# Plain values of two batches in 18 tiles of 128 rows, their queries in token order, sums over tiles in PSUM

## The chip, the cores and the metric

The kernel runs as one program on one core of a Trainium2 chip. The metric is device time in microseconds, median of several runs; lower is better. Three runs of the kernel before took 307.17 us in the median (306.58 to 307.39). One profiled execution gives the times of its instructions; its own time was 307.09 us, and the span from its first to its last instruction 305.2 us.

A core has five engines with queues of their own: PE (matmul), DVE (vector), ACT (activation), POOL (general) and SP, which here only issues transfers. Matmul results land in PSUM, in eight banks of 128 partitions by 512 fp32; PE, DVE and ACT reach it.

## The reference

Attention of 8 batches, 8 heads, 576 tokens and 64 dimensions, with two kinds of mask, then a two-layer product with a leaky ReLU:

```python
mask_plain = (rel >= 0) & (rel < window)                                   # window 32, heads 0 to 3
mask_dil = (rel >= 0) & (rel < window * dilation) & (rel % dilation == 0)  # dilation 4, heads 4 to 7
attn = exp(masked scores / 8), divided by its sum over keys
x = (attn @ v), heads side by side: 4608 tokens x 512
out = leaky_relu(x @ w_in) @ w_out      # w_in 512 x 2048, w_out 2048 x 512, fp32 in and out
```

A plain query sees its own token and the 31 before it; a dilated query sees 32 tokens four apart, which are 32 neighbours among the tokens of the same residue by 4.

## The kernel before, in words

**Chunks.** `x` is kept transposed in fp16 in `xt`, 1152 columns for two batches, token order by residue (column r*96 + i stands for token 4i + r). Twelve chunks of 384 columns follow each other: `up` (L1073) multiplies a chunk by `w_in` in 16 groups of four matmuls, ACT applies the leaky ReLU on the way to `gt` (L1084), and the product with `w_out` gives 128 tokens at a time. The first four such tiles are plain products (`down`, L1244, four steps of four matmuls of 512 columns); the others go in groups of four with seven products in place of eight (L1335). The last four chunks form the up product in the same way (`up_seven`, L1157). Chunks 0 and 1 are the first 384 tokens of batch 0 and of batch 1, chunk 2 the rest of both.

**Attention of batches 0 and 1** (`EARLY`) works on pairs of heads: hp 0 and 1 plain, hp 2 and 3 dilated. `load_group` loads q, k, v of four heads in fp32, casts them (L342 on ACT, L344 on the others) to `nat` and `v_all`; `turn` transposes q and k by PE (L729) and moves them from PSUM to `slots` (`move`, L646 on ACT, L648 on DVE): queries to `qbd`, where the two heads stand in halves with zeros between, so that one matmul gives both heads' scores, and keys to `kt`. Tokens are cut in part 0 (the first 384) and part 1 (the rest); the dilated heads' last tokens come by `load_rest`. `unit` does 192 queries of two heads:

- scores into one bank of `sps` or `hps` (L888; L872 for the short dilated ones). In part 0 (`BY_PE`) a matmul of the identity with a bias (L869) comes first and adds -60000 outside the mask; in part 1 a multiplication after the exponential (L905) does that;
- exponential by ACT (L894) into one of four `ee` tiles;
- values (L929, L949, L939) and sums into a bank of `ops`. In part 0 (`TILED`) one matmul gives 64 rows, head by head on the two halves of the array, and the sums come from a stationary of ones (L917); in part 1 the stationary has values and ones side by side;
- the reciprocal by ACT as exp(-ln) (L961, L963), and the normalization by DVE into `xt` (L967).

For the plain heads the queries are in blocks of 96 and each block has the 128 keys that it can see, from 32 before it. Neighbouring key blocks overlap by 32 rows, so the values are loaded in 12 pieces of 128 rows every 96 rows for each pair of heads; in a block of 96 the queries stand residue by residue. For the first block of batch 0 the rows before token 0 are filled by a memset (`t_vz`) and two extra transfers.

**Attention of batches 2 to 7** (`late_unit`, L1010 scores, L1023 exponential, L1026 mask, L1016 sums and values, L1034, L1037 reciprocal, L1045 normalization) is spread over the rest of the span; its transposes are by DVE into `turned` (L697) or `slots` (L704, L717, L722), with copies by POOL (L687).

**The order of the work** is planned. Every operation is a task with an engine (or a choice of engines), a duration assumed by the author, dependencies and a priority; `_Plan.run` places them one after the other, `latest` recomputes the priorities backward, and `SEEDS` disturbs them at random in some passes. The instructions are written out in the planned order, one in-order queue for each engine, all loads and stores on SP. `FIRST` is the order of the early loads: b and c are q, k of batches 0 and 1 (dilated heads first), v and y their values, i an eighth of `w_in`, o an eighth of `w_out`, 0 and 1 the rest of each batch. `WHEN`, `RANKS`, `MOE`, `SUMS`, `W_SUMS`, `NEAR` are times that set priorities. In gaps of the plan before 62 us PE multiplies zeros (L1558); eight such matmuls (L1454) open the program. The pieces of `w_out` are staged in `xt1`, `wst` and `gt1`, some of them twice, so that a later one waits for the casts of an earlier.

Of the kernel before, what the change touches and what calls it, by code (L numbers as in the profile page):

```python
# [19 lines left out]
WHEN = (4.52, -1.03, 5.19, 90.96, 96.86, 93.61, 150.56, 174.24)  # L20
WARM = 62.0
W_SLOW = 1.25
SEEDS = (0, 0, 0, 0, 0, 0, 0, 0, 0, 775539)
AFTER = -1495.0
NEAR = -1498.63
FIRST = 'bvbviiii0iiiicycyoooooooo1'
RANKS = ((12.88, -25.12), (25.21, -10.26), (-1.14, 23.42), (33.7, 4.07))


def _constants():  # L30
# [3 lines left out]
    key = p - 32  # L34
    c = np.arange(96)[None, :]
    qry = 4 * (c % 24) + c // 24
    rel = qry - key
    band = (rel >= 0) & (rel < WIN)
    first = band & (key >= 0)
    rel0 = c - p  # L40
    d0 = (rel0 >= 0) & (rel0 < WIN)
# [3 lines left out]
    masks = np.concatenate([d0, first, band, d2], axis=1)  # L45
# [165 lines left out]
def kernel(  # L211
# [51 lines left out]
    NBIAS, NMASK = 3 * 96 + 48, 96 + 48  # L263
    NCON = 128 + NBIAS + NMASK
    NLATE = 480 + 2 * 384
    M_D0, M_FIRST, M_BAND, M_KEEP = 128, 224, 320, 128 + NBIAS
# [92 lines left out]
    def zeros(n):  # L359
# [6 lines left out]
    t_con = add("ACT", 0.21, 0.22, [t_bias],  # L366
                lambda e: nc.scalar.activation(out=con[:, M_KEEP:NCON], in_=con[:, M_BAND:M_KEEP], func=AF.Exp),
                -700)
# [38 lines left out]
    t_vz = clear("POOL", vst[1][0:PAD, 0:D], 0.1, 0.0, -9350)  # L407
# [17 lines left out]
    def load_group(b, g, prio, prio_v):  # L425
# [39 lines left out]
        elif early:  # L465
            lv = []
            for j in range(2):
                n = 12 - (first and j == 0)
                lj = [load("SP", at(vs, 0, 128, (12 * j + 12 - n) * D, [D, n], [1, D]),
                           dram(v, base + (1152 * j + 96 * (12 - n) - 32) * D, [D, 128], [96 * D, n],  # L470
                                [1, D]), 128 * n, 256, v_old, prio_v + 0.3 * j)]
                if n < 12:
                    lj += [load("SP", at(vs, PAD, 128, 0, [1, D]), dram(v, 0, [D, 96], [1, D]),
                                96, 256, v_old, prio_v), t_vz]
                lv.append(lj)
# [18 lines left out]
        for j in range(2):  # L494
# [20 lines left out]
            n_v = 256 if dil else 384  # L515
            h_a, h_s = j * n_v, 2 * n_v
            n, w = n_v // D, 128 * (8 if dil else 6)
# [10 lines left out]
    def load_rest(b, prio):  # L528
# [5 lines left out]
        for o, src in ((0, q), (1, k)):  # L534
            lo.append(load("SP", at(st, 0, 128, o * 256, [1, 256]),
                           dram(src, b * H * HS + 512 * D, [HS, 8], [4 * D, 16], [1, 256]),
                           128, 1024, s_old, prio))
# [1083 lines left out]
```

## Time and profile before

| what | value |
| --- | --- |
| median of three runs | 307.17 us |
| the profiled execution | 307.09 us, span 305.2 us |
| PE busy | 293.0 us (96%), 3039 matmuls |
| DVE busy | 249.9 us (82%) |
| ACT busy | 225.1 us (74%) |
| POOL busy | 118.8 us (39%) |
| PE, DVE, ACT busy in 20 to 40 us | 17.31, 16.47, 18.01 |
| in 40 to 60 us | 19.40, 13.71, 13.39 |
| in 60 to 80 us | 20.00, 14.21, 17.49 |
| in 80 to 100 us | 19.81, 19.40, 17.84 |
| first matmul with w_out (L1244) | 46.49 us |
| first up matmul of chunk 1 | 54.82 us |

An engine's busy time is the sum of its instructions' spans without double counting. Matmuls are pipelined: one of 192 columns lasts 0.245 us by itself, while a row of eight takes 0.66 us, so the distance from start to start tells what one costs. In a timeline row the columns are start, length from the first start to the last end, engine, line, operation, tiles, shape and count, and in brackets the idle time before it and what ended that. In the stretches the columns are the window, its length, the busy time of PE, PE's weight loads, DVE, ACT and POOL with their counts, the granted clock, the share of the transfer engines and GB/s. The chain of waits has start, length and what it was.

### The profile page before, as it was taken

To read this page: it belongs to the slowest core of one execution; us is meant where nothing else is said; L and a number is where in the kernel's file an instruction comes from. 1 tells how busy PE (TensorE), PEld (TensorE's weight loads), DVE (VectorE), ACT (ScalarE), POOL (GpSimd) and SP (SyncE) were. 2 spreads that over 40 slices of the span, in tenths; PEclk is the share of its full clock that TensorE was granted. 3 is DMA by queue.
4 is the path that set the end of the run, shared out by engine and by line. 5 is a ranking of instruction groups with operands and counts; after the bars stand their busy time and mean duration, and the time that the engine had idled before them with its cause. 6 is when DMAs were issued, how large, how long until landed. Compare 5 with 4: busy or idle time off the path is not lost.

```text
span 305.2 us, 8114 instructions
## 1 busy us (share of the span) xinstructions
PE 293.0 (96%) x3039; PEld 230.5 (76%) x3039; DVE 249.9 (82%) x477; ACT 225.1 (74%) x549; POOL 118.8 (39%) x164
## 2 busy tenths in 40 slices
PE   8788889999999999999999999999999999999994
PEld 4444544566898778778777787778999999999983
DVE  6778785749899989998998899999998868586842
ACT  4989985789898885787677778667568888777420
POOL 6148643058936826936845753771000000000000
PEclk9999999999999999999999999999999999999998
DMA  7999999899799697757994898782212110121034
GB/s 248 336 320 393 312 378 200 171 180 202 173 174 195 134 173 157 138 130 141 177 159 138 148 189 153 143 175 78 73 55 80 42 37 0 37 71 35 11 111 123
DMA packets 157159, 47.22 MB, mean 155 GB/s; under 512 B 137408, under 2 KB 154560, under 8 KB 157120
## 3 DMA queue, kind: packets, MB, share of 16 engines
q1 hardware_dynamic: 156544, 46.39, 64.6%
q8 instruction: 24, 0.39, 0.6%
q10 hardware_dynamic: 576, 0.32, 0.4%
q14 instruction: 15, 0.12, 0.1%
HBM read 37.24 MB, written 9.44 MB: 153 GB/s over the span
## 4 chain that ended last, share of the span: by engine, by line
PE 78%; DVE 6%; ACT 5%; DMA 4%; SPq 3%; issue 1%; DVEq 0%
PE hps L1073 22%; PE fps L1335 21%; PE tp L1335 8%; PE hps L1157 7%; PE fps L1244 5%; PE ops L1016 4%; PE ops L1157 3%; DMA wst<-in_moe_w_in_dram 3%; SPq L333 3%; PE sps L1157 2%; ACT gt L1084 1%; PE sps L1010 1%; PE sps L1016 1%; DVE ee L1026 1%; PE ops L1010 1%
## 5 line engine op out<-in xcount | busy, mean ns | idle before, releaser
L1073 PE MATMUL hps<-xt,w_in 128*128 128x384 f16 (+1 forms) x556 | 97.6, 307 | 1.7 <-DVE w_in L344 1.2
L1335 PEld LDWEIGHTS <-gt 128*128 128x128 f16 x768 | 72.3, 98 | 9.0
L1084 ACT ACTIVATE gt<-hps 128x384 f16<-128x384 f32 (+1 forms) x139 | 62.2, 455 | 22.6 <-PE hps L1073 21.3
L1073 PEld LDWEIGHTS <-w_in 128*128 128x128 f16 x576 | 50.1, 98 | 25.4 <-ACT w_in L342 1.8
L1335 PE MATMUL fps<-w_out,gt 128*128 128x256 f16 x368 | 47.2, 272 | 0.0
L687 POOL COPY slots<-turned 64x512 f16<-64x512 f16 (+1 forms) x36 | 25.7, 715 | 41.2 <-DVE turned L697 34.8
L344 POOL CAST v_all<-vst 64x1152 f16<-64x1152 f32 (+3 forms) x29 | 34.8, 1201 | 7.6 <-DMA vst<-in_v_dram 6.9
L344 POOL CAST nat<-stg 128x576 f16<-128x576 f32 (+1 forms) x44 | 33.8, 789 | 8.0 <-DMA stg<-in_k_dram 3.6
L1026 DVE TENSOR_TENSOR ee<-ee,late_m 128x384 f16<-128x384 f16 (+1 forms) x48 | 29.0, 619 | 3.8 <-ACT ee L1023 3.5
L1045 DVE TENSOR_TENSOR xt<-ops,rc 128x288 f16<-128x288 f32 x48 | 26.5, 553 | 3.7 <-PE ops L1016 2.3
L1157 PEld LDWEIGHTS <-w_in 128*128 128x128 f16 x256 | 21.8, 98 | 0.4
L1364 ACT COPY stg<-fps 128x512 f32<-128x512 f32 (+1 forms) x24 | 12.7, 530 | 11.9 <-PE fps L1335 11.8
L1037 ACT ACTIVATE rc<-rc 128x288 f32<-128x288 f32 x48 | 20.9, 447 | 0.6
L717 DVE STREAM_TRANSPOSE slots<-nat 64x576 f16<-64x576 f16 x24 | 18.4, 767 | 0.4
L697 DVE STREAM_TRANSPOSE turned<-nat 128x576 f16<-128x576 f16 (+1 forms) x24 | 17.5, 735 | 0.4 <-ACT nat L342 0.2
L1157 PEld LDWEIGHTS <-stg 128*128 128x128 f16 x192 | 16.6, 98 | 0.3
L1321 DVE TENSOR_TENSOR gt<-gt 128x1024 f16<-128x1024 f16 x21 | 16.2, 773 | 0.6 <-PE fps L1335 0.6
L1016 PEld LDWEIGHTS <-v_all 128*128 128x128 f16 x240 | 14.5, 98 | 3.0 <-issue 0.2
L1016 PE MATMUL ops<-ee,v_all 128*128 128x96 f16 (+2 forms) x240 | 16.4, 199 | 0.1
L1335 PE MATMUL fps<-wst,gt 128*128 128x256 f16 x128 | 16.4, 273 | 0.0
L967 DVE TENSOR_TENSOR xt<-ops,rc 64x192 f16<-64x192 f32 (+1 forms) x30 | 10.6, 352 | 6.9 <-ACT rc L963 6.4
L1244 PE MATMUL fps<-w_out,gt 128*128 128x512 f16 x64 | 16.1, 380 | 0.0
(151 smaller groups left out, 594.2 us busy)
## 6 DMA issues: line engine op xcount, KB each, us to landing
stg<-in_q_dram SPq DMA_DIRECT2D x48, 144.0 KB, 3.4
stg<-in_k_dram SPq DMA_DIRECT2D x48, 144.0 KB, 3.1
vst<-in_v_dram SPq DMA_DIRECT2D x12, 288.0 KB, 4.1
vst<-in_v_dram SPq DMA_DIRECT2D x24, 128.0 KB, 2.7
gt<-in_moe_w_in_dram SPq DMA_DIRECT2D x5, 512.0 KB, 8.2
xt<-in_moe_w_out_dram SPq DMA_DIRECT2D x3, 512.0 KB, 5.7
gt<-in_moe_w_out_dram SPq DMA_DIRECT2D x3, 512.0 KB, 8.0
vst<-in_v_dram SPq DMA_DIRECT2D x3, 384.0 KB, 6.0
```

What stands on the lines that cost most here:

```text
L344: ENG[e].tensor_copy(out=dst, in_=src)
L687: lambda e: (nc.scalar.copy if e == "ACT" else nc.gpsimd.tensor_copy)(out=at(to, p0, p1, p0 if to is qb else 0, *dims), in_=at(fr, p0, p1, ...
L717: lambda e, p0=64 * h: nc.vector.transpose(at(qb, p0, p0 + 64, p0, [128, 9], [1, 64]), na[p0:p0 + 64, S:2 * S]), prio))
L1016: nc.tensor.matmul(at(bk, 0, 128, o, *dims), stationary(s), et[:, c:c + n], start=i == 0, stop=i == len(parts) - 1, skip_group_check=True)
L1026: lambda e: nc.vector.tensor_tensor(out=et[:, 0:w], in0=et[:, 0:w], in1=mk, op=ALU.mult), prio + 0.1)
L1037: lambda e: nc.scalar.activation(out=rt[:, 0:NQ], in_=rt[:, 0:NQ], func=AF.Exp, scale=-1.0),
L1045: lambda e: nc.vector.tensor_tensor(out=dst, in0=at(ot, 0, 128, 0, *src), in1=at(rt, 0, 128, 0, *src), op=ALU.mult), prio + 0.2)
L1073: nc.tensor.matmul(ht[:, 0:n], at(w_in, 0, 128, i * DFF + j // 2 * 256 + j % 2, [2, 128]), at(xt[m % 2], 0, 128, i * 1152 + x0 + x, [1, n] ...
L1084: lambda e: nc.scalar.activation(out=gt[c % NG][:, j * n_c + x:j * n_c + x + n], in_=ht[:, 0:n], func=AF.Prelu, alpha=0.01),
L1157: nc.tensor.matmul(bk[:, 192 * jj:192 * jj + 192], w(i, 2 * jp + jj), x(i), start=first and jj == 0 and i == 0, stop=jj == 1 and i == 1, s ...
L1244: nc.tensor.matmul(ft, g[:, j * n_c + tt * 128:j * n_c + tt * 128 + 128], w_out[:, j * DM:j * DM + DM], start=(j == 0), stop=(j == NJ - 1))
L1335: nc.tensor.matmul(bk[:, x:x + HN], tl[:, off + j * step:off + j * step + 128], rhs(j), start=first and x == 0 and j == 0, stop=j == HJ - ...
```

## The change

The plain heads of batches 0 and 1 are cut otherwise. The four heads' 2304 value rows are loaded once each: for each pair of heads 9 tiles of 128 rows, so that of two adjacent heads (576 rows each) the one has four whole tiles and half of the fifth, and the other the second half of it and four whole ones. The queries stand in token order. A unit of 192 queries takes two or three key tiles (`segs_u`: index, block, first key, rows from and to, first query, number of queries, column in the mask); a query that sees keys in two tiles has scores in both, so the columns of a unit are 448 or 512 instead of 384, and values and sums are added up over the tiles in PSUM. A tile can be half (64 rows).

With it go: masks of other shapes and three activations instead of one to make them; the exponential tile of every early unit is now one of the three `turned` tiles (ring E0) instead of one of four `ee`; in token order the query moves and the normalization read PSUM with a step of 4 elements or of 128; two query moves of a pair become one; the memset and the extra transfers for the first block go; and the durations and times of the plan are set anew, with another order of the early loads (`FIRST`) and other passes (`SEEDS`).

```diff
-WHEN = (4.52, -1.03, 5.19, 90.96, 96.86, 93.61, 150.56, 174.24)
+WHEN = (9.76, -9.78, 7.23, 85.46, 112.41, 84.21, 128.59, 158.08)
-W_SLOW = 1.25
-SEEDS = (0, 0, 0, 0, 0, 0, 0, 0, 0, 775539)
+W_SLOW = 1.5
+SEEDS = (0, 0, 0, 0, 0, 0, 0, 0, 0, 382976, 459246, 239349)
-NEAR = -1498.63
-FIRST = 'bvbviiii0iiiicycyoooooooo1'
-RANKS = ((12.88, -25.12), (25.21, -10.26), (-1.14, 23.42), (33.7, 4.07))
+NEAR = -1473.8
+FIRST = "bvbviiii0iiiicoocoyoooooy1"
+RANKS = ((28.17, -29.18), (37.15, -3.52), (9.85, 51.56), (73.19, -0.03))
...
-    MOE = 36.21
+    MOE = 27.44
...
         elif early:
...
+            lv = [load("SP", at(vs, 0, 128, 576 * j, [D, 9], [1, D]),
+                       dram(v, base + 2 * j * HS, [D, 128], [128 * D, 9], [1, D]),
+                       1152, 256, v_old, prio_v + 0.3 * j) for j in range(2)]
...
-            cs = [[192, 2], [24, 4], [1, 24]] if not dil else [[step, xs[0][1]], [1, n]]
+            cs = [[1, 4], [4, 48]] if not dil else [[step, xs[0][1]], [1, n]]
...
-            elif lo == 0:
-                o, od, id_ = 0, [[96, n // 24], [24, 4], [1, 24]], [[24, n // 24], [128, 4], [1, 24]]
             else:
-                o, od, id_ = 360 + lo, [[24, 4], [1, n]], [[128, 4], [1, n]]
+                o, od, id_ = 4 * lo, [[4, n], [1, 4]], [[1, n], [128, 4]]
...
-                for lo, hi in ((0, 128),) if dil else ((0, 120), (120, 128)):
-                    q_users += q_to((lo, lo), lo, hi, [tq])
+                q_users += q_to((0, 0), 0, 128, [tq])
...
-        en, e_old = ring("E", NE, e_users := [])
+        segs_u = ((), (), ()) if dil else (
+            ((0, 0, 0, 128, 0, 160, 0), (1, 128, 0, 128, 128, 64, 0)),
+            ((1, 128, 0, 128, 192, 96, 64), (2, 256, 0, 128, 256, 128, 0)),
+            ((2, 256, 0, 128, 384, 32, 128), (3, 384, 0, 128, 384, 160, 0), (4, 512, 0, 64, 512, 64, 0))
+        ) if hp == 0 else (
+            ((0, 0, 64, 128, 0, 96, 160), (1, 64, 0, 128, 64, 128, 0)),
+            ((1, 64, 0, 128, 192, 32, 128), (2, 192, 0, 128, 192, 160, 0), (3, 320, 0, 128, 320, 64, 0)),
+            ((3, 320, 0, 128, 384, 96, 64), (4, 448, 0, 128, 448, 128, 0)))
+        segs_u = segs_u[u]
+        W = 384 if dil else 2 * sum(x[5] for x in segs_u)
+        en, e_old = ring("E0", len(turned), e_users := [])
...
+            if not dil:
+                if by_pe:
+                    for i, (x, _, _, _, _, _, n, c) in enumerate(segments()):
+                        nc.tensor.matmul(at(st, 0, 128, x, [W // 2, 2], [1, n]), ident,
+                                         at(con, 0, 128, M_BAND + c, [0, 2], [1, n]),
+                                         start=i == 0, stop=False, skip_group_check=True)
+                for i, (x, _, key, a, z, q0, n, _) in enumerate(segments()):
+
+                    for a, z in ((a, z),) if by_pe or z - a == 128 else ((0, 64), (64, 128)):
+                        nc.tensor.matmul(at(st, a, z, x, [W // 2, 2], [1, n]), kb[:, PAD + key:PAD + key + z - a],
+                                         at(qb, 0, 128, q0, [S, 2], [1, n]), start=not by_pe,
+                                         stop=not by_pe or i == len(segs_u) - 1, skip_group_check=True)
+                return
...
+            if not dil:
+                for hh in range(2):
+                    out, p0 = (ot[64 * hh:64 * hh + 64, :], 0) if tiled else (ot, 192 * hh)
+                    for own in (True, False) if tiled else (True,):
+                        for i, (x, blk, _, a, z, q0, n, _) in enumerate(segments()):
+                            c = (hh * 6 + blk) * 128
+                            o = q0 - 192 * u + (p0 if own else 192)
+                            nc.tensor.matmul(out[:, o:o + n],
+                                             vt[a:z, c:c + (D if tiled else 128)] if own else ones[a:z, :],
+                                             et[a:z, hh * W // 2 + x:hh * W // 2 + x + n],
+                                             start=i == 0 and own and (tiled or hh == 0),
+                                             stop=i == len(segs_u) - 1 and (not own if tiled else hh == 1),
+                                             skip_group_check=True)
+                return
```

## The prediction

> **What bounds the kernel now.** I read the page's sums first, then busy time by stretches, then the chain of waits, and last the instructions in order of time for the first 60 us.
>
> ```profile
> PE 293.0 (96%) x3039; PEld 230.5 (76%) x3039; DVE 249.9 (82%) x477; ACT 225.1 (74%) x549; POOL 118.8 (39%) x164
> ```
>
> PE's 96% hides two different stages, which the stretches separate:
>
> ```profile
> 20.00:40.00 20.00, 17.31 (x140) 9.74 (x141) 16.47 (x41) 18.01 (x42) 13.96 (x22) 1.00 1.04 348
> 60.00:80.00 20.00, 20.00 (x185) 13.44 (x184) 14.21 (x32) 17.49 (x46) 14.20 (x23) 1.00 1.02 187
> 80.00:100.00 20.00, 19.81 (x261) 17.84 (x259) 19.40 (x33) 17.84 (x50) 11.62 (x14) 1.00 0.89 178
> ```
>
> From 60 us on PE is full; in 80 to 100 us DVE is nearly full too. Before that PE's busy time is made of latencies and of matmuls on zeros (L1558). So I price PE by start to start. In the chain eight matmuls of 384 columns take 1.30 us, of 192 0.66, of 256 0.87:
>
> ```profile
> 54.98 1.30 PE hps L1073 x8
> 220.47 0.66 PE hps L1157 x8
> 293.85 5.24 PE fps L1335 x48
> 299.09 1.76 PE ops L1335 x16
> ```
>
> That is 163, 82 and 109 ns, so N columns cost N/2.4 + 2.5 ns (28 ns at least, from the spacing of the 32-column ones). At these prices all matmuls but those on zeros make 274.5 us. PE ends at 300.85, so 26.3 us of PE's time are lost, and 4.4 us follow its end. Summing the timeline's PE rows, 20.2 us of work are done by 42.7 us (22.5 lost), 34.9 by 60 us (25.1 lost); after 60 us only 1.2 us are lost. The end is therefore: PE's work + what it loses, nearly all before 60 us + 4.4.
>
> What PE waits for early is ACT and DVE. The chain lies on ACT, almost unbroken, from 22.17 us (a part of w_in lands at 22.14) to 42.65: casts of w_in, evictions L1084, exponentials. The first w_out matmul (L1244) stands at 46.49, though w_out's first parts landed at about 38.4:
>
> ```profile
> 37.19 0.83 POOL L344 CAST v_all<-vst 128x768 f16<-128x768 f32 x1 [0.93 <-DMA vst<-in_v_dram]
> 38.47 0.61 POOL L344 CAST w_out<-xt 128x512 f16<-128x512 f32 x1 [0.46 <-DMA xt<-in_moe_w_out_dram]
> 45.95 0.33 PE L888 MATMUL sps<-slots 128*128 128x192 f16 x2
> 46.20 0.28 PE L929 MATMUL ops<-ee,v_all 128*64 128x96 f16 x4
> 46.31 0.25 PE L917 MATMUL ops<-ee,ones 128*64 128x192 f16 x2
> 46.49 1.04 PE L1244 MATMUL fps<-w_out,gt 128*128 128x512 f16 x4
> ```
>
> These last four rows give two more prices. A plain unit's values take 0.11 + 0.08 = 0.19 us for 768 columns, because matmuls of 64 output rows stand in pairs on the two halves of the array. And each passage between 128- and 64-row matmuls loses 0.09 to 0.10 us: 46.20 - 45.95 is 0.25 where two matmuls need 0.165; 46.49 - 46.31 is 0.18 where 0.08 is needed.
>
> **PE work added.** Per batch there are four tiled plain units (bias and sums by PE) and two that are masked. Score columns of a unit go from 384 to 448, in one tiled and one masked unit to 512. Bias and scores of the tiled ones: 0.327 to 0.383 (three) and 0.44 (one), +0.28. Their values: the loop now runs one head through all its blocks and sums before the other head, so neighbours share a half and pair only at the one change: 896 columns are 0.393 less 0.03, 1024 are 0.43; 3 x 0.36 + 0.43 - 4 x 0.19 = +0.75. Masked units: scores +0.085, values +0.11. Together 1.23 a batch, 2.45 for both: 277.0. Bounds: +1.1 if values pair as now, +2.6 with no overlap; I take 2.45, the rows' own rate.
>
> The Trainium skill, TensorE: Matmul & The Clock Gate, Part 3 (the mechanism), says that tiles overlap when they lie on different strips and that matmuls start and end in order. The rows of L929 and L917 agree; by that rule the added 1.5 us of values over both batches stay, and by pairing as now the sum would be 1.3 us less.
>
> **Passages.** The order of the built program has 53 changes of tile shape where there are 26, since blocks of 64 keys now alternate with blocks of 128. From the first w_out matmul on there are 24, against 12 in the same part of before: 12 x 0.095 = +1.1 us. No row shows a matmul on 64 input rows, so the bounds are 0 and 1.2; I take 1.1, by the nearest row.
>
> The Trainium skill, TensorEngine Tiling (Array Packing), Key Properties, says that a change of tiling mode drains TensorE and a change of tile does not. The 0.09 to 0.10 us rows agree for columns; by the rule the 64-row blocks cost the same, and if they did not the sum would be 1.1 us less.
>
> **What is gained early.** In the order of SP two parts of w_out come ahead of batch 1's plain queries and all eight ahead of its plain values. Successive w_out parts land 1.25 us apart (POOL's casts at 42.08, 43.36, 44.61, 45.84), 512 KB each, so at that rate the first two land near 32, the last near 43.4 and the plain values near 45. SP's 5.3 us wait on DVE's w_out cast goes, as POOL now makes both casts of that part. The values are used after 32.6 us of PE work, about 53 us: 8 us of cover. The plain V itself shrinks from 768 to 576 KB a batch, 0.5 us of that rate; batch 0's cast (15.31 us) moves up so much, but a ring of three instead of four exponential tiles makes the fourth plain unit wait for the first one's values, which eats it. I cost it at nothing; w_in's landing and ACT are next.
>
> PE's order now interleaves: the first w_out matmul follows 20.4 us of work, where before it followed 22.6. By its groups' durations ACT has 31.0 us of instructions up to the 14th eviction L1084 where it had 33.5 (fewer of batch 1's exponentials come first); at before's idle that is 39.8 us instead of 42.3. But DVE gets dearer, which sizes alone don't show:
>
> ```profile
> 6.18 0.42 DVE L648 COPY slots<-fps 128x512 f16<-128x512 f16 x1
> 13.52 0.68 DVE L648 COPY slots<-fps 128x512 f16<-128x512 f16 x1
> 78.60 0.45 DVE L1045 TENSOR_TENSOR xt<-ops,rc 128x288 f16<-128x288 f32 x1
> 89.21 0.68 DVE L1045 TENSOR_TENSOR xt<-ops,rc 128x288 f16<-128x288 f32 x1 [0.37 <-PE ops L1016]
> ```
>
> The second of each pair reads PSUM with a step (plain keys; plain late units), the first without. Token order puts such steps into 16 normalizations (0.23 x 192/288 = 0.15 each, 2.4 us) and three query copies on DVE (0.27 each, 0.8), and four masks widen (0.2): +3.4 us, against six small copies of 0.18 gone, split over ACT and DVE. Up to the point in question DVE has 1.9 of it, and was idle 2.4 us in 22 to 40 us; I let half of the 1.9 through: first w_out matmul near 40.9 (bounds 39.5 and 42). Lost so far: 40.9 - 20.4 = 20.5.
>
> **The sum.** 20.5 + 24 passages (2.3) + waits and the last filler, as between 46.5 and 60 us of before (0.7) + after 60 us as before (1.2) = 24.7 lost, against 26.3. End: 277.0 + 24.7 + 4.4 = 306.1 against 305.2 (the last eight blocks of PE and the stores behind them stand in the same order). The profiled execution took 307.09, 1.9 more than its span, and lies 0.08 under the median 307.17; so 308.1 by the median.
>
> **Rivals.** (1) Faster: the early start pays in full. ACT alone sets the first w_out matmul (39.5, lost 19.1) and 64-row blocks drain nothing (-1.1): lost 22.2, end 303.6, time 305.5. For it: w_out lands early, and PE's queue has 17 us of work at hand from there. Against: DVE's 16.47 of 20 us in 20 to 40. (2) No change: one of the two comes true, 306.6 to 308.0. It includes that loading V once brings nothing as V never ended the wait for long (0.93 us at 37.19). (3) DVE becomes the bound. At the fourteenth unit of the late batches DVE has 87.1 us of work behind it now and 88.3 in the changed order (84.9 by its groups' durations and the 3.4), PE 87.9 and 89.6. PE is there at 87.9 + 25.6 = 113.5 now; if DVE keeps all its idle time (24.3 us in the first 120), PE is there 1.2 later, at 114.7, and has lost 25.1, with the 0.5 after it 25.6: end 307.0, time 308.9; with the plain chain at 53 to 58 us held up by the ring of three tiles, some 2 us more. It decides when less than 0.9 us of the 3.4 goes into idle time. For it: DVE's 19.40 of 20 us in 80 to 100; against: 14.21 in 60 to 80.
>
> **Numbers.** Forecast, slower by 0.3 to 0.6%: 0.32, rival 3 0.18, rival 2 0.23, rival 1 0.27. So slower 0.50, same 0.23, faster 0.27; 0.3% (0.9 us) is about what a measurement here can tell. The range must leave out no more than 0.1 on each side: from 305.3, in rival 1, to 311.0, in rival 3. The slower cases alone: 308.1 to 311.
>
> **What would show it.** The first w_out matmul near 41 us and the first matmul of chunk 1's up product near 60, where it was 54.82 with less work behind it; tiled values of 0.36 to 0.43 us and gaps near 0.1 at 64-row blocks; normalizations of 0.5 us; PE lost about 25 us in all. The forecast is wrong if the first w_out matmul stands at 39 or earlier, if the 64-row blocks follow without gaps, or if after 60 us PE waits for DVE by more than 2 us.

## The result, and the profile after

The changed kernel took 310.27 us in the median of six runs (309.91 to 312.86); the kernel before, on the same chip in the same session, 306.75 us. The ratio is 1.0131 with a 95% interval of 1.0093 to 1.0169: slower by 1.3%. The prediction said slower, 308.1 us, with 305.3 to 311.0 as its range. The sign is right and the time lies in the range, but the loss is nearly four times the one that was forecast (0.9 us): 3.5 us by the medians (1.1%), 3.1 us by the spans of the two profiled executions (305.2 and 308.3), 4.0 us by the ratio, which compares means and so takes in the one run of 312.86 us.

The page's sum of busy times, to be held against the line shown of before:

```profile
PE 295.0 (96%) x3078; PEld 232.8 (76%) x3078; DVE 249.3 (81%) x471; ACT 225.8 (73%) x545; POOL 121.2 (39%) x169
```

PE is busy 2.0 us longer and no other engine by more than 2.4. As before, the sum does not show where. Busy time by stretches of the changed kernel, with the same columns as before (start and end, length, then busy time and instructions of PE, PEld, DVE, ACT, POOL, granted clock, DMA share, GB/s):

```profile
20.00:40.00 20.00, 15.39 (x127) 8.47 (x124) 15.02 (x37) 15.84 (x36) 13.04 (x22) 1.00 1.05 395
60.00:80.00 20.00, 19.79 (x157) 12.28 (x157) 13.33 (x31) 16.14 (x40) 12.10 (x23) 1.00 0.98 184
80.00:100.00 20.00, 19.83 (x277) 18.68 (x275) 17.89 (x33) 17.23 (x55) 12.83 (x16) 1.00 0.86 171
```

In 20 to 40 us all three engines do less than before (PE 15.39 against 17.31, DVE 15.02 against 16.47, ACT 15.84 against 18.01). In 60 to 80 us PE has 157 matmuls where it had 185, though it is called 99% busy. DVE did not become the bound: it has 17.89 of 20 us in 80 to 100, where it had 19.40.

The instructions in order of time (start, length, engine, line, operation, output and input, count; in brackets the idle time before and what ended it) show the two marks that the prediction had named, the first `w_out` matmul (now L1271) and the first up matmul of chunk 1 (now L1100):

```profile
43.39 1.03 PE L1271 MATMUL fps<-w_out,gt 128*128 128x512 f16 x4
...
61.16 0.34 PE L888 MATMUL sps<-slots 128*128 128x96 f16 x4
61.34 1.03 PE L1271 MATMUL fps<-w_out,gt 128*128 128x512 f16 x4
62.20 0.38 PE L1585 MATMUL fps<-warm 128*128 128x512 f16 x1
62.78 0.33 PE L888 MATMUL sps<-slots 128*128 128x96 f16 x4 [0.21 <-ACT turned L905]
62.95 0.81 PE L1100 MATMUL hps<-xt,w_in 128*128 128x384 f16 x4
```

The `w_out` product starts at 43.39 us, 3.1 us earlier than before but 2.5 later than forecast (40.9); the up product of chunk 1 at 62.95, forecast near 60. Between them a new hole: a filler (L1585) and a wait on ACT ahead of a dilated score.

The chain of waits (start, length, what) shows why the first mark is late. Before, it ran through the landing of `w_in`:

```profile
12.49 9.65 DMA wst<-in_moe_w_in_dram
...
22.17 0.34 ACT w_in L342
```

In the changed kernel it runs through batch 0's plain heads instead, reciprocal by reciprocal (L988, L990) and at the end through two casts of `w_in` on DVE (L340), up to their last normalization (L994), behind which the up product of chunk 0 stands:

```profile
19.24 0.26 ACT rc L988
19.52 0.37 ACT rc L990
...
20.85 0.42 DVE w_in L340
21.30 0.72 DVE w_in L340
22.06 0.50 DVE xt L994
22.60 0.32 PE tp L1100
```

In the kernel before, that normalization began at 19.34 us, right behind its reciprocal:

```profile
19.34 0.36 DVE L967 TENSOR_TENSOR xt<-ops,rc 128x192 f16<-128x192 f32 x1 [0.18 <-ACT rc L963]
```

In the changed kernel the second step of its reciprocal also stands behind a cast of `w_in`, on ACT:

```profile
20.78 0.62 ACT L338 CAST w_in<-gt 64x512 f16<-64x512 f32 x1
21.42 0.36 ACT L990 ACTIVATE rc<-rc 128x192 f32<-128x192 f32 x1
```

Pricing the matmuls as in the prediction (columns/2.4 + 2.5 ns, two halves of the array side by side; in the two units of 64-row blocks one matmul after the other), PE's account of the two profiled executions is:

| | before | after | difference |
| --- | --- | --- | --- |
| lost up to the first `w_out` matmul | 23.84 us | 23.47 | -0.4 |
| lost after it | 2.64 | 4.77 | +2.1 |
| PE's work | 274.4 | 276.2 | +1.8 |
| from PE's end to the end of the span | 4.38 | 3.89 | -0.5 |

The four differences make 3.1 us before rounding, the difference of the spans. The last row tells little: over the profiled executions of all runs it lies between 3.2 and 4.4 us. By stretches PE loses 21.7 us before and 23.4 after up to 40 us, then 3.4 and 1.6 up to 60, then 0.0 and 2.1 up to 80, then 1.4 and 1.2.

### The profile page after: what moved, and what is told of

The parts are those of the page before. It is cut to its first block, busy times and chain, and to the rows that moved or that the text cites. A ratio compares the mean times of both kernels' runs of the same rounds, so it can differ in the third digit from the quotient of the medians.

```text
span 308.3 us, 8181 instructions
## 1 busy us (share of the span) xinstructions
PE 295.0 (96%) x3078; PEld 232.8 (76%) x3078; DVE 249.3 (81%) x471; ACT 225.8 (73%) x545; POOL 121.2 (39%) x169
## 4 chain that ended last, share of the span: by engine, by line
PE 83%; ACT 6%; DVE 5%; DMA 2%; issue 2%; SPq 1%; POOL 0%; ACTq 0%; DVEq 0%
PE hps L1100 23%; PE fps L1362 22%; PE tp L1362 8%; PE hps L1184 7%; PE ops L1043 4%; PE fps L1271 4%; PE ops L1184 3%; DMA vst<-in_v_dram 2%; DVE slots L637 2%; PE sps L1184 2%; ACT gt L1111 1%; PE sps L1037 1%; PE ops L1037 1%; PE sps L1043 1%; ACT slots L635 1%
## 5 line engine op out<-in xcount | busy, mean ns | idle before, releaser
L1100 PE MATMUL hps<-xt,w_in 128*128 128x384 f16 (+1 forms) x556 | 95.9, 307 | 1.4 <-DVE w_in L340 1.2
L1111 ACT ACTIVATE gt<-hps 128x384 f16<-128x384 f32 (+1 forms) x139 | 61.3, 455 | 20.0 <-PE hps L1100 18.3
L1100 PEld LDWEIGHTS <-w_in 128*128 128x128 f16 x576 | 50.2, 98 | 23.8 <-issue 1.9
L340 POOL CAST v_all<-vst 64x1152 f16<-64x1152 f32 (+3 forms) x29 | 33.2, 1144 | 12.8 <-DMA vst<-in_v_dram 9.1
L340 POOL CAST nat<-stg 128x576 f16<-128x576 f32 (+1 forms) x46 | 36.8, 824 | 2.0 <-DMA stg<-in_q_dram 1.6
L1072 DVE TENSOR_TENSOR xt<-ops,rc 128x288 f16<-128x288 f32 x48 | 26.9, 560 | 5.5 <-PE ops L1043 3.7
L1053 DVE TENSOR_TENSOR ee<-ee,late_m 128x384 f16<-128x384 f16 (+1 forms) x48 | 26.5, 564 | 2.6 <-ACT ee L1050 2.1
L1348 DVE TENSOR_TENSOR gt<-gt 128x1024 f16<-128x1024 f16 x21 | 17.1, 828 | 0.7 <-PE fps L1362 0.6
L994 DVE TENSOR_TENSOR xt<-ops,rc 64x192 f16<-64x192 f32 (+1 forms) x30 | 12.1, 418 | 5.3 <-ACT rc L990 5.1
L1271 PE MATMUL fps<-w_out,gt 128*128 128x512 f16 x64 | 16.3, 379 | 0.0
L1043 PEld LDWEIGHTS <-sides 128*128 128x128 f16 x240 | 14.0, 98 | 2.6 <-issue 0.2
```

The costliest lines, as they stand in the source:

```text
L340: ENG[e].tensor_copy(out=dst, in_=src)
L1043: nc.tensor.matmul(at(bk, 0, 128, o, *dims), stationary(s), et[:, c:c + n], start=i == 0, stop=i == len(parts) - 1, skip_group_check=True)
L1053: lambda e: nc.vector.tensor_tensor(out=et[:, 0:w], in0=et[:, 0:w], in1=mk, op=ALU.mult), prio + 0.1)
L1072: lambda e: nc.vector.tensor_tensor(out=dst, in0=at(ot, 0, 128, 0, *src), in1=at(rt, 0, 128, 0, *src), op=ALU.mult), prio + 0.2)
L1100: nc.tensor.matmul(ht[:, 0:n], at(w_in, 0, 128, i * DFF + j // 2 * 256 + j % 2, [2, 128]), at(xt[m % 2], 0, 128, i * 1152 + x0 + x, [1, n] ...
L1111: lambda e: nc.scalar.activation(out=gt[c % NG][:, j * n_c + x:j * n_c + x + n], in_=ht[:, 0:n], func=AF.Prelu, alpha=0.01),
```

## The experiments

All ratios are to the kernel before, run beside. The spans of one kernel scatter by 1 us and more (303.0 to 306.5 us in 29 runs of the kernel before), so a verdict rests on the ratio, and the profiled executions only show the place. Each ratio is known to about 0.25%, the one of the changed kernel to 0.4%. The kernels of runs 2, 3, 4, 10 and 11 leave out the order in which the blocks expect their queries or values (the eleventh some keys too): they price a part of the change and cannot replace it.

### 1 to 4: blocks of 64 rows, the step of the reads, and the loading of V

In the first, the values and sums of every block run over all 128 rows (`values`, plain branch):

```diff
                             o = q0 - 192 * u + (p0 if own else 192)
+                            a, z = 0, 128
```

> The 64-row blocks are multiplied over all 128 rows (the rows added are zero in the exponentials), in the same order of instructions. Theory P, that the passages between 64- and 128-row matmuls cost the time: the two units of 1.3 us (17.76 and 59.83 us) fall to about 0.25 us, 1.05 us each, the two masked units with such a block lose about 0.25 us each; the first of them lies in batch 0's chain, so the second matmul of chunk 0's up product (22.60 us) comes 0.7 to 1.1 us earlier, the first w_out matmul at 42.4 to 42.8 us instead of 43.39, and the whole kernel is 1.8 to 2.6 us faster than the changed kernel: about 308. Rival S, that batch 0's chain is late for its stepped copies and normalizations: the first unit's 1.05 us only goes into idle time, chunk 0's up product stands within 0.3 us of 22.6, and the gain is about 1.3 us, that of the units after 30 us.

Measured: 1.0109 (1.0085 to 1.0134). The unit with 64-row blocks in the changed kernel, in order of time:

```profile
59.83 0.40 PE L931 MATMUL ops<-turned,v_all 64*64 64x96 f16 x2
60.16 0.40 PE L931 MATMUL ops<-turned,ones 64*64 64x96 f16 x2
60.49 0.40 PE L931 MATMUL ops<-turned,v_all 64*64 64x96 f16 x2
60.82 0.40 PE L931 MATMUL ops<-turned,ones 64*64 64x96 f16 x2
61.16 0.34 PE L888 MATMUL sps<-slots 128*128 128x96 f16 x4
```

What follows the same unit with whole rows, in the first run:

```profile
59.48 0.33 PE L888 MATMUL sps<-slots 128*128 128x96 f16 x4
59.65 1.03 PE L1272 MATMUL fps<-w_out,gt 128*128 128x512 f16 x4
60.52 0.38 PE L1586 MATMUL fps<-warm 128*128 128x512 f16 x1
62.17 0.33 PE L888 MATMUL sps<-slots 128*128 128x96 f16 x4 [1.28 <-ACT turned L905]
```

Eight matmuls that took 1.33 us (59.83 to 61.16) take 0.48 from 59.00, passage to the next shape included. The execution is 0.61 us ahead at this place, so without the edit the next `w_out` matmul would stand at 60.73; it stands at 59.65, 1.08 us earlier (0.85 from the shorter unit, the rest because it starts while the unit ahead of it still runs). But the score behind it comes at 62.17, which is 62.78 - 0.61: the gain is swallowed whole by the wait for ACT. In batch 0's chain nothing is gained either: from the last cast of its plain queries and keys to the last normalization it is 9.97 us (11.42 to 21.39), with 64-row blocks 9.82. Theory P falls as to the place; here the passages cost PE 1.1 us, and the time no more than can be told (1.0131 to 1.0109, the intervals overlap) while ACT is late behind them.

In the second, query copies and normalizations read PSUM without a step:

```diff
-                o, od, id_ = 4 * lo, [[4, n], [1, 4]], [[1, n], [128, 4]]
+                o, od, id_ = 4 * lo, [[n, 4], [1, n]], [[128, 4], [1, n]]
...
-            cs = [[1, 4], [4, 48]] if not dil else [[step, xs[0][1]], [1, n]]
+            cs = [[48, 4], [1, 48]] if not dil else [[step, xs[0][1]], [1, n]]
```

> Query copies and normalizations of the plain heads of batches 0 and 1 read PSUM without a step, in the same order of instructions; the queries then lie in another order than the blocks assume, so the outputs of these heads are wrong. Theory S, that the step makes batch 0's chain late: copies of 64x384 fall from 0.57 to 0.36 us and normalizations from 0.49 to 0.36 us, the first plain scores come at 13.4 instead of 13.89 us, the second matmul of chunk 0's up product 0.6 to 1.0 us earlier than 22.60, and the kernel 1 us faster than the changed one. Theory P (the 64-row passages do it): the rows fall as said, but the up product moves by less than 0.5 us and the time by less than 0.5 us.

Measured: 1.0099 (1.0073 to 1.0124). The rows of DVE in order of time:

```profile
12.21 0.74 DVE L637 COPY slots<-tp 64x384 f16<-64x384 f16 x2
...
20.93 0.36 DVE L994 TENSOR_TENSOR xt<-ops,rc 128x192 f16<-128x192 f32 x1 [0.37 <-ACT rc L990]
```

The two copies take 0.74 us together where they took 1.14, the normalization 0.36 instead of 0.49, and the plain chain 9.16 us instead of 9.82. The rows are as theory S expected. So is the time, about 1 us less (1.0131 to 1.0099), but the two intervals overlap; the later pairs of runs with and without steps give 0.4% (first and third) and 0.5% (seventh and tenth). The third run has both edits.

> Both edits at once, same order of instructions, outputs of the plain heads of batches 0 and 1 wrong as with the copies alone. If passages and steps together are where the early gain went, chunk 0's second up matmul stands at 21 us or earlier, the first w_out matmul at 41.5 to 42 us, and the time is 3 to 3.6 us under the changed kernel, at 306.7 to 307.3, level with the kernel before. If the rest is the wider exponentials and the ring of three tiles, the up product stays above 21.5 us and the time above 308.

Measured: 1.0068 (1.0046 to 1.0090). The second up matmul stands at 20.66 us, and the first `w_out` matmul only at 42.70; of the 3 to 3.6 us expected about 1.9 came (1.31% less 0.68%). Passages and steps are about half of the loss, not all of it.

In the fourth, V is loaded in as many bytes as before:

```diff
-            lv = [load("SP", at(vs, 0, 128, 576 * j, [D, 9], [1, D]),
-                       dram(v, base + 2 * j * HS, [D, 128], [128 * D, 9], [1, D]),
+            lv = [load("SP", at(vs, 0, 128, 768 * j, [D, 12], [1, D]),
+                       dram(v, base + 2 * j * HS, [D, 128], [96 * D, 12], [1, D]),
```

> The plain values of batches 0 and 1 are loaded as many times as before (24 blocks of 128 rows at a step of 96, 768 KB a batch instead of 576 KB), all else as in the changed kernel and in its order; the values are then those of other rows, so the outputs of these heads are wrong. If loading V once is hidden, as the prediction said (cast at 13.87 us, used at 16.86 us; later used at 56.5 us): w_out and V land 0.5 us later per batch and the time is within 0.4 us of the changed kernel. If the smaller load is what carries the early start, the first w_out matmul comes 0.5 to 1 us later and the time is 0.5 to 1.2 us longer.

Measured: 1.0113 (1.0084 to 1.0141), the same as the changed kernel within what can be told. So the part of the change that its name speaks of, loading V once, brings no time: nothing that sets the time waited for these bytes. In this execution the second up matmul stood at 21.54 us, against 22.60, with more bytes to load: so much do the landings of the first loads differ between executions.

### 5 and 6: blocks and order apart

The constants of the order were exchanged between the two kernels (`FIRST`, `WHEN`, `RANKS`, `NEAR`, `W_SLOW`, `MOE`, `SEEDS`, `W_SUMS`, `SUMS`); here two of them as they stand in the fifth run:

```diff
-MOE = 27.44
-FIRST = "bvbviiii0iiiicoocoyoooooy1"
+MOE = 36.21
+FIRST = 'bvbviiii0iiiicycyoooooooo1'
```

> The new blocks with the order constants of the kernel before (FIRST, WHEN, RANKS, NEAR, W_SLOW, MOE, SEEDS and the two weights of the sums); the order is planned anew from them, w_out again lands after batch 1's plain queries and values, the first w_out matmul follows 24.8 us of PE's work instead of 21.6. Theory C, the blocks alone cost what was measured (1.8 us of PE's work, 0.8 us in the plain chain, the passages) and the order brings nothing: 1.0 to 1.5% over the kernel before, as the changed kernel. Theory O, that the early w_out does bring the 3 us that the prediction gave it and the blocks cost 6 to 7 us: 2% over the kernel before or more. Theory R, that the new order itself is the loss: within 0.7% of the kernel before.

> The kernel before with the order constants of the changed kernel and nothing else: old blocks of 96 queries, V loaded as before, w_out early (the first w_out matmul follows 20.8 us of PE's work instead of 24.4). Theory C: within 0.4% of the kernel before. Theory O: 0.7 to 1.1% faster, the first w_out matmul at 41 to 42 us instead of 46.5. Theory R: 0.7% slower or more, with PE waiting after 60 us.

Measured: new blocks in the old order 1.0157 (1.0132 to 1.0183), old blocks in the new order 1.0077 (1.0051 to 1.0104). No theory fits both. The new order is good for the new blocks by 0.3%, if at all (1.0157 to 1.0131, the intervals overlap), and bad for the old ones by 0.8%. That early `w_out` brings its 3 us in any blocks falls clearly (the whole order was exchanged, so what `w_out`'s place alone is worth stays open): in the old blocks it does start the product at 42.80 us instead of 46.49, and PE then has one tile's step and waits, for POOL's casts of the next parts among others:

```profile
42.80 1.03 PE L1244 MATMUL fps<-w_out,gt 128*128 128x512 f16 x4
...
45.27 0.61 PE L729 MATMUL tp<-con,nat 128*128 128x128 f16 x8 [0.63 <-POOL w_out L344]
...
47.42 0.81 PE L1244 MATMUL fps<-w_out,gt 128*128 128x512 f16 x3
```

By 80 us that kernel has lost 26.9 us of PE's time, the kernel before 25.1. An earlier first instruction of a product says little while what feeds the second is not earlier too.

### 7 and 8: the copies of the last rows, and the step on the other side

The wait on ACT at 62 us goes back to eight copies of 64x128 (the last sixteen rows of queries and keys of each head), which alternate between ACT and DVE. In the changed kernel, ACT:

```profile
58.56 0.71 ACT L635 COPY slots<-tp 64x128 f16<-64x128 f16 x2
59.79 0.26 ACT L635 COPY slots<-tp 64x128 f16<-64x128 f16 x1 [0.51 <-DVE slots L637]
60.40 0.26 ACT L635 COPY slots<-tp 64x128 f16<-64x128 f16 x1 [0.35 <-DVE slots L637]
61.02 0.26 ACT L635 COPY slots<-tp 64x128 f16<-64x128 f16 x1 [0.36 <-DVE slots L637]
...
62.24 0.49 ACT L905 ACTIVATE turned<-sps 128x384 f16<-128x384 f32 x1
```

Each waits for the one before it on the other engine, and behind them stand two reciprocals and the exponential that frees the bank for the score at 62.78. In batch 0 the same eight stand on the chain of waits from 28.11 to 30.46 us. The edit (on top of whole rows), where these copies are made:

```diff
                                         [tq] + zq + zk + (busy if dil and o else []), prio))
+                        new[-1].fn = lambda e, f=new[-1].fn: f("DVE")
```

> Whole rows as in the first of these runs, and the eight copies per batch of the last sixteen rows of queries and keys (64x128, at 28 and 58.6 us) all made by DVE where they alternate between ACT and DVE, each waiting for the other; the order of the matmuls is the same. If it is this alternation that holds ACT and with it the two dilated scores at 59.5 and 62.2 us (PE idle or on a filler from 60.5 to 62.2 in the whole-row run), the eight take 1.6 to 1.8 us instead of 2.7, PE's loss between 60 and 65 us falls from 1.8 to 0.7 us or less, and the time is 0.8 to 1.5 us under the whole-row run (1.0109 of before), near 1.007. If ACT's own work of normalization and exponentials sets that place, PE's loss stays above 1.4 us and the time where it is.

Measured: 1.0058 (1.0033 to 1.0084), 0.5% under the whole-row run. DVE makes the eight in a row, which the rows of DVE show:

```profile
58.63 2.33 DVE L637 COPY slots<-tp 64x128 f16<-64x128 f16 x8
```

The rows of PE in the same run have the score 1.4 us earlier than at 62.78, though this execution is only 0.1 us ahead at 57 us:

```profile
61.12 0.38 PE L1587 MATMUL fps<-warm 128*128 128x512 f16 x1
61.34 0.33 PE L889 MATMUL sps<-slots 128*128 128x96 f16 x4
```

The eight copies take longer than expected in sum, but ACT is free of them. PE's loss from 60 to 65 us falls from 1.8 to 1.0 us, less than said, and the time by what was said. That window alone proves little, as executions are shifted against it: the fourth run, whose copies alternate, has 1.0 us there too. From 40 to 80 us PE loses 2.8 us here, 3.5 in the whole-row run and 3.9 in both the changed kernel and the fourth run.

The eighth run moves the step of the second run to the write, with the same values in the end:

```diff
-                o, od, id_ = 4 * lo, [[4, n], [1, 4]], [[1, n], [128, 4]]
+                o, od, id_ = 4 * lo, [[1, 4], [4, n]], [[128, 4], [1, n]]
...
-            xs = [[nu, 4], [1, n]] if not dil else [[nu, 2 if u < 2 else 4], [1, n]]
+            xs = [[1, n], [nu, 4]] if not dil else [[nu, 2 if u < 2 else 4], [1, n]]
```

> Whole rows, the copies by DVE, and the step of query copies and normalizations moved from their read of PSUM to their write to SBUF (same values, so the outputs are the reference's). If the step on the read is what costs (64x384 copies 0.57 against 0.36 us, normalizations 0.49 against 0.36), a step on the write is free: rows as in the run without steps, batch 0's last plain normalization 0.7 us earlier than without this edit, and a ratio to before of 1.003 to 1.005. If any step costs, the rows stay at 0.5 us and more and the time equals that of the run with whole rows and DVE copies.

Measured: 1.0546 (1.0511 to 1.0582). Neither expectation holds; a step on the write is far dearer than on the read:

```profile
12.87 2.04 DVE L637 COPY slots<-tp 64x384 f16<-64x384 f16 x2 [0.41 <-ACT slots L635]
...
21.86 1.11 DVE L996 TENSOR_TENSOR xt<-ops,rc 128x192 f16<-128x192 f32 x1 [0.99 <-ACT rc L992]
23.45 1.11 DVE L996 TENSOR_TENSOR xt<-hps,rc 128x192 f16<-128x192 f32 x1
```

A copy takes 1.0 us (0.37 without a step, 0.56 with it on the read), a normalization 1.11 us (0.36 and 0.49). The last plain normalization stands at 27.02 us (21.50 in the seventh run), the first `w_out` matmul at 50.44 (43.19): what is added to batch 0's chain goes through to PE.

### 9: the same copies in the kernel before

The edit of the seventh run alone, in the kernel before.

> The kernel before with one edit: the eight copies per batch of the last sixteen rows of queries and keys all made by DVE. If the gain that this edit gave in the changed kernel (ratio 1.0109 to 1.0058, with whole rows in both) belongs to the place that the new order gives these copies, the kernel before, which has eight up products of chunk 1 ahead of the scores that wait for them (54.98 to 56.3 us) and loses nothing between 60 and 80 us, stays within 0.3%. If the alternation costs PE wherever it stands, it is 0.3 to 0.6% faster than the kernel before, and that would be the fastest version here.

Measured: 0.9993 (0.9974 to 1.0013). No change. Two things are different there, and the run does not part them: the up products of chunk 1 stand ahead of the scores that wait, and the eight copies change engine only three times (ACT three from 56.76 us, DVE one, ACT one, DVE three up to 59.07, 2.3 us in all), where in the changed kernel they change six times in 2.7 us. So sharing these copies between ACT and DVE is older than the change; the new order made them alternate more often and took their cover away.

### 10 and 11: the causes together

The tenth run has whole rows, copies by DVE and reads without a step at once, the three diffs above.

> The changed kernel with whole rows, the copies by DVE, and query copies and normalizations without a step (outputs of the plain heads of batches 0 and 1 wrong, as in the run without steps). If the three causes add: 1.0058 less about 0.3%, a ratio to before of 1.001 to 1.004, and PE's loss up to 40 us at 22.5 us or less, against 21.7 in the kernel before and 23.4 in the changed one. If the plain chain is held by something else once the copies are out of the way, the ratio stays at 1.005 or above.

Measured: 1.0011 (0.9987 to 1.0036), level with the kernel before. PE's loss up to 40 us is 21.2 us, and the `w_out` product starts where the prediction had put it:

```profile
40.45 0.65 PE L1102 MATMUL hps<-xt,w_in 128*128 128x384 f16 x3
40.93 1.03 PE L1273 MATMUL fps<-w_out,gt 128*128 128x512 f16 x4
```

In the eleventh the queries that see two blocks see one:

```diff
-        W = 384 if dil else 2 * sum(x[5] for x in segs_u)
+        cut = []
+        for k, key, a, z, q0, n, c in segs_u[::-1]:
+            to = cut[0][4] if cut and cut[0][4] > q0 else q0 + n
+            if cut and cut[0][4] == q0:
+                cut[0] = (*cut[0][:4], q0 + n, cut[0][5] - n, cut[0][6] + n)
+            cut.insert(0, (k, key, a, z, q0, min(n, to - q0), min(c, 127) if n == 32 else c))
+        segs_u = tuple(cut)
+        W = 384
```

> As the one before, and the blocks no longer overlap: each plain unit has 384 score columns instead of 448 or 512, the queries that see two blocks see one, and the mask is 96 columns repeated (outputs of these heads wrong in this too); instructions and their order are the same. It takes away the added PE work that is left (about 0.56 us a batch: bias and scores 0.35, values 0.21) and 0.06 to 0.1 us of each of twelve exponentials. If wider units are the last of the cost, the ratio falls by 0.3 to 0.5%, to 0.997 to 1.001: then whole rows, copies, steps and width together are the difference to the kernel before. If it stays at 1.003 or above, what is left lies in the order of the work (PE's loss after 40 us and the chain of batch 0).

Measured: 0.9970 (0.9949 to 0.9992). PE's work is 274.65 us, 1.1 less than in the tenth, as expected, and the plain chain of batch 0 takes 8.54 us (8.98 in the tenth). Its profiled execution shows it less well than the ratio: the span is 304.4 us, 303.9 in the tenth, and the first `w_out` matmul stands at 41.87. Taken out one after the other, in this order, the ratios give 0.2% for the rows (not to be told from nothing by itself), 0.5% for the copies, 0.5% for the steps, 0.4% for the width, 1.6% in all; each is known to 0.3 to 0.5%, and only the steps were measured in more than one place. With all four taken out, what is left of the change is 0.3% faster than the kernel before.

### 12: the step on PE's write

The last run keeps the outputs and takes the step out of the normalizations by having PE write the values and sums 48 columns apart, on top of whole rows and copies by DVE:

```diff
-                            o = q0 - 192 * u + (p0 if own else 192)
+                            o = q0 // 4 - 48 * u + (p0 if own else 192)
...
-                            nc.tensor.matmul(out[:, o:o + n],
+                            nc.tensor.matmul(at(ot, lo, hi, o, [1, n // 4], [48, 4]),
```

> The changed kernel with whole rows, the copies by DVE, and the step of the plain normalizations moved to PE: the values and sums are written to PSUM 48 columns apart, so that the normalization reads it without a step; query copies keep theirs; the outputs are the reference's. If PE writes with a step as fast as without, eight tiled matmuls take 0.22 us from start to start as before, normalizations 0.36 instead of 0.49 us, and the ratio to before is 1.002 to 1.005, under the 1.0058 of the same kernel without this edit. If a step on PE's write costs as it did on DVE's write (1.11 against 0.49 us), the units take 0.4 us or more and the ratio is 1.007 or above.

Measured: 1.0119 (1.0099 to 1.0138), 0.6% over the seventh run. One unit, and the first row of the next, in order of time:

```profile
16.17 0.39 PE L933 MATMUL ops<-turned,v_all 128*64 128x160 f16 x4
16.36 0.40 PE L933 MATMUL ops<-turned,ones 128*64 128x160 f16 x4
16.55 0.40 PE L933 MATMUL hps<-turned,v_all 128*64 128x96 f16 x4
```

From start to start a unit takes 0.38 us, without the step 0.22. The Trainium skill, PSUM — Partial Sum Buffer, Specifications, says that a pattern that is not contiguous slows matmuls significantly; these rows agree, at a factor of 1.7. The normalizations do fall to 0.36 us, and batch 0's plain chain is still 9.9 us (9.8 in the seventh run). The step costs in each of the three places tried, and least on DVE's read, where the changed kernel has it. No version with the reference's outputs beat the kernel before; the best of them with the new blocks is the seventh, 1.0058.

## Why the prediction was right and wrong

**Sign and range.** Both held, in part by luck. The forecast time is 2.2 us short (308.1 against 310.27), and the range reached up to 311.0 only for the rival in which DVE becomes the bound, which did not come true.

**The early gain: the step that failed.** The prediction let the time up to the first `w_out` matmul shrink by 3.4 us of PE's loss (23.9 to 20.5); it shrank by 0.4, and that matmul at 43.39 us lies outside the bounds given for it (39.5 and 42). The sentence at fault is the one on batch 0's plain values, "I cost it at nothing; w_in's landing and ACT are next". It asked when V lands, and there it was right (fourth run), and whether a ring of three eats that gain. But the plain chain behind it got longer in itself, and that was costed on DVE's sum ("up to the point in question DVE has 1.9 of it", half let through) and not on the chain. From the last cast of plain queries and keys to the last normalization it is 7.8 us before (11.51 to 19.34) and 9.8 after (12.24 to 22.06). The runs give 1.3 of these 2.0 us to steps, rows and width together (8.54 us are left in the eleventh): 0.7 to 1.0 to the steps, 0.4 to the width. What the last 0.7 us are was not tested, but the record points to the new order. Its casts of `w_in` at the end of the chain (two on DVE, one on ACT, shown above) hold the last normalization back by about 0.9 us: without them the rows would let it start at 20.78 + 0.36, near 21.1 instead of 22.06 (an estimate; before, one such cast on ACT held the last reciprocal for about 0.3). And the sixth run, old blocks in the new order, with four exponential tiles and no step, has a chain of 8.53 us (11.43 to 19.96), the same 0.7 over the kernel before, so the ring of three is not needed for it; but there the values wait for V's cast instead, so the equal sum may be chance. The other 0.7 us by which the chain ends later were there at its start, no more than what executions of the same instructions differ by there (9.68 us in the changed kernel for ACT's cast of queries, 9.08 and 8.92 in two of the runs). The cover named, the landing of `w_in`, does not stand on the changed kernel's chain.

**After the first w_out matmul.** Forecast +1.8 us of loss, of it 1.1 for passages; measured +2.1. The sum is near, for another reason in part: the passages do drain (0.11 to 0.12 us at each change of rows), but the place where they were dearest was covered by the eight copies between ACT and DVE, which the prediction did not look at. It expected PE to lose nothing new between 60 and 80 us; it lost 2.1.

**PE's work.** Forecast +2.45 us, measured +1.8. The tiled plain values were taken as serial, 0.36 to 0.43 us a unit, because the program runs one head through all its blocks before the other. They take 0.22:

```profile
16.86 0.30 PE L931 MATMUL ops<-turned,v_all 128*64 128x160 f16 x4
16.98 0.28 PE L931 MATMUL ops<-turned,ones 128*64 128x160 f16 x4
17.08 0.29 PE L931 MATMUL hps<-turned,v_all 128*64 128x96 f16 x4
17.18 0.29 PE L931 MATMUL hps<-turned,ones 128*64 128x96 f16 x4
17.40 0.28 PE L1585 MATMUL fps<-warm 128*128 128x256 f16 x1
```

Each of the first two rows has the values, and then the sums, of both heads, though in the program both stand for one head first. The bound "if values pair as now" (+1.1) was the nearer to the truth: with whole rows PE's work is 1.4 us over the kernel before, and the other 0.4 of the 1.8 are the two units of 64-row blocks, whose matmuls do not stand side by side.

**The rivals.** That early `w_out` pays in full is out, and the sixth run shows an order with early `w_out` that loses time in the old blocks. That 64-row blocks drain nothing is out. DVE did not become the bound by its sum (third rival): it has less to do in 80 to 100 us than before. That rival's side remark did look at a plain chain, but at batch 1's at 53 to 58 us and at the ring of three tiles; the one that counted was batch 0's.

**DVE's rows.** Normalizations of 0.49 to 0.50 us and query copies of 0.57 are what was said (0.36 and 0.15 more; 0.27 more was said for the copies, 0.2 came). Their size at the first mark was near, too (0.95 us let through, 0.7 to 1.0 in batch 0's chain), though by DVE's sum and not by the chain; by the ratios they are 0.3 to 0.5% of the time. What the sum did not have is the rest of the chain's 2.0 us and the copies between ACT and DVE.

## What to carry to other kernels

Before a chain of small operations is costed at nothing, add up its own length before and after, latency by latency; where it has just lost its cover, 0.1 us on each of a dozen operations becomes the time. When an order is planned anew, look for waits that the old order hid, such as copies that hop between two engines, and not only at what was changed. A transfer that nothing waited for brings nothing when it shrinks, and a layout that saves bytes is paid for in steps, wider units and odd shapes at each later place that reads it.

## What the runs showed of the hardware

- Matmuls of 64 output rows on the two halves of the array ran beside each other although four of one half stood ahead of four of the other in the program: 896 columns in 0.22 us, where 896/2.4 is 0.37. The Trainium skill, TensorE: Matmul & The Clock Gate, Part 3 (the mechanism), says that matmuls start and end in the order of the program; the rows of 16.86 to 17.18 us above disagree, as the starts of the two heads' matmuls alternate.
- Matmuls on 64 and on 128 input rows in alternation start 0.157 to 0.174 us apart at 96 and 128 columns (the unit at 59.83 us), for which 0.04 to 0.06 would do by the prices above.
- A step between neighbouring elements: a 64x384 copy by DVE from PSUM takes 0.37 us without, 0.56 with a step of 128 elements on the read, 1.0 with one of 4 on the write to SBUF; a 128x192 normalization takes 0.36 without, 0.49 with a step of 4 on the read, 1.11 with one of 96 on the write. With a step of 48 on PE's write to PSUM eight matmuls go from 0.22 to 0.38 us.
